# The last chunk's rows turned by TensorE, the early experts' loads on SP alone, and new ranks for the planner, in a fused mLSTM, FFN and MoE kernel

## The chip, the cores and the metric

The kernel runs on one core of a Trainium2 chip. The metric is the device time of one execution in microseconds. Of the kernel before there are three timed runs, with a median of 672.15 us (670.86 to 674.29), and one more execution with a profile.

## The reference

Three layers follow each other. With B = 4 sequences, H = 8 heads, S = 768 steps and D = 40 there are 3072 tokens of 320 values.

```
# 1. mLSTM, per batch and head, over the steps t
m_new = max(f_t + m, i_t);  f' = exp(f_t + m - m_new);  i' = exp(i_t - m_new)
C = f' * C + i' * outer(v_t, k_t);   n = f' * n + i' * k_t
y_t = sigmoid(o_t) * (C @ q_t) / max(|n . q_t|, 1)
x = y as [3072, 320]
# 2. FFN: w_in [320, 2048], w_out [2048, 320]
h = x @ w_in;   x = (h * sigmoid(h)) @ w_out
# 3. MoE, top 1 of 8 experts: w1 [8, 320, 1024], w2 [8, 1024, 320]
e = argmax(x @ w_gate);   p = softmax(x @ w_gate)[e]
out = p * (relu(x @ w1[e]) @ w2[e])
```

All values are float32.

## The kernel before, in words

**Tiles.** The sequence is cut into six chunks of 128 steps, and a unit is one chunk of one sequence: unit t = 4c + b, so units 20 to 23 are the last chunk. A unit loads K, Q, V and the gates, makes scores and values on TensorE in the chunkwise form of the recurrence, and ends with a tile of 128 tokens, written as two f16 halves (a high and a low part) into `yy`. The FFN wants that tile turned, tokens along the free axis. `turned` (L624) does it: for t below 3 by six TensorE transposes (L636) and a copy (L638), else by one DMA transpose on SP's queue (L628). K and Q of all chunks but the first are turned by L628 too.

**FFN.** `l1(t, g)` takes a quarter of the 2048 columns in two halves of 16 products each (L1018, 128x512 of PSUM in all). ScalarE makes tanh of it (L1020), VectorE the gate product (L1022), ScalarE casts the high f16 part (L1025), and VectorE or GpSimd makes the low part (L1026). `l2(t, g)` then takes twelve products with `w_out` (L1047 to L1049) into one bank, and after the fourth quarter ScalarE moves the tile out (L1053).

**Route.** After each chunk `route(c)` scales its four tiles into f16 rows (L1102 on ScalarE, L1105 on GpSimd, L1106 on VectorE), turns each row block by a DMA transpose on SP (L1110), takes the gate logits on TensorE (L1122), and finds for each token its expert and its place among that expert's tokens (up to L1151). GpSimd then sends the tokens' rows by indirect DMA (L1177) to their places in a table in HBM, `rows_x`.

**Experts.** A slot is 128 tokens of one expert: `fetch_slot` (L1252, L1253) brings them in turned by a DMA transpose, and `slot` multiplies them by the expert's w1 (L1279), applies relu (L1281, L1283), multiplies by w2 (L1292 to L1294), weights them (L1297) and writes them out (L1309). Seven slots of experts 0 to 2 are early: they hold tokens of the first five chunks alone and run beside the end of the FFN and the last route. Then come 18 static slots, and three extra slots whose expert is known only at run time. An expert's weights come in quarters. `load_e` (L1190) issues four DMAs for a quarter (L1201 to L1204, 704 KB in all) into a stage, of which there are two at first. ScalarE and VectorE convert the stage into f16 halves: L1215 and L1228 on ScalarE, L1219, L1223 and L1230 on VectorE. A quarter is named (e, g) below, expert and quarter. The issue of a load with a fixed expert may go on SP's queue or on ScalarE's.

**What sets the order.** The program is first recorded as operations with engine, duration, tiles read and written, and a rank (L1 to L281). A list scheduler then runs over all operations forward and backward eight times with these durations, and keeps the round with the earliest planned end. The instructions of every engine are emitted in the order of that plan. At run time each engine works off its own list in order, with semaphores between engines, and the queues of SP and ScalarE hold their DMA issues in the same order. The ranks of the operations are built from constants in `RK` (L28), so another constant or another duration can move any instruction of any engine.

**What the change touches.** `RK`; `turned`; the call of `turned` for K, Q and `yy` in `unit`; L1110 in `route`; the engine choice in `load_e`, by `load_all`; four of the planner's durations.

Of the kernel before, what the change touches and what calls it, by code (L numbers as in the profile page):

```python
# [25 lines left out]
SWG = 32.0  # L26
EX = 4
RK = dict(  # L28
    tiles=19.85, win=310.54, dwin=120.43, wout=56.12, dwout=-21.22, u0=-372.07, u1=-36.9, u2=-978.22, u3=-878.97,
    lead1=113.09, lead=1032.66, l1c=-437.46, l2c=-463.45, l2=-163.58, gates=-736.39, load=-73.54, state=-65.11, route=-284.86,  # L30
)


# [254 lines left out]
def mlstm_moe_kernel(ctx, tc, q, k, v, ig, fg, og, w_in, w_out, w_gate, w1, w2, out):  # L288
    nc = tc.nc
    B, H, S, D = q.shape  # L290
# [17 lines left out]
    def op(*args, **kw):  # L308
        plan[0].op(*args, **kw)
# [91 lines left out]
    we_b = []  # L401
# [219 lines left out]
    def src(x, c, b):  # L621
        return x[b, :, c * CH:(c + 1) * CH, :].rearrange("h p d -> p h d")

    def turned(t, a, z, n, rank):  # L624

        flat = a.ap[:, 0:n * 128] if len(a.ap.shape) == 2 else a.ap.rearrange("p x c -> p (x c)")
        if t >= B - 1:
            op("SP", 1300, lambda: sp.dma_start_transpose(out=z.ap, in_=flat), R=[a], W=[z], rank=rank,  # L628
               lag=2800, move=212 * n)
            return  # L630
        ps, kk = bank("at", 128, 512)
        ps = ps.bitcast(F16)[:, 0:n * 128].rearrange("p (x c) -> p x c", c=128)

        def go():
            for x in range(n):
                pe.transpose(ps[:, x, :], flat[:, x * 128:(x + 1) * 128], ident16)  # L636
        op("PE", 70 * n, go, R=[a, "ident"], W=[kk], rank=rank)
        op(AD, ad(128 * n), lambda m: (m.copy if m is ac else m.tensor_copy)(out=z.ap, in_=ps), R=[kk], W=[z], rank=rank)  # L638

    def unit(t):  # L640
# [42 lines left out]
        def whole_turned(a, z, r):  # L683

            flat = a.ap.rearrange("p h d -> p (h d)")
            ps, kk = bank("at", 128, 512)

            def go():
                for i in range(4):
                    x = slice(i * 128, (i + 1) * 128)  # L690
                    pe.transpose(ps[:, x], flat[:, x], ident)
            op("PE", 4 * 110, go, R=[a, "ident"], W=[kk], rank=r)
            op(AD, ad(512), lambda m: (m.copy if m is ac else m.tensor_copy)(out=single(z), in_=ps),
               R=[kk], W=[z], rank=r)

# [3 lines left out]
        if c == 0:  # L699
            whole_turned(kr, kT, p)  # L700
            whole_turned(qr, qT, p + 0.5)
        else:
            halves(kr.ap, kr, k4[:, :, 0::2, :], k4[:, :, 0, :], k4[:, :, 1, :], K, p)
            turned(t, K, kT, H, p)
            halves(qr.ap, qr, q4[:, :, 0:2, :], q4[:, :, 0, :], q4[:, :, 2, :], Q, p + 0.5)
            turned(t, Q, qT, H, p + 0.5)

        def exps(h, x):
            ac.activation(  # L709
# [3 lines left out]
        for g in range(2):  # L713
            if c == 0:
                ps, kk = bank("at", 128, 4, CH)

                def first(g=g, ps=ps):
                    pe.matmul(ps, idb.ap, mneg.ap, start=True, stop=False)
                    for j in range(4):
                        h = b * H + 2 * j + g  # L720
                        one = sel.ap[:, h:h + 1].to_broadcast([128, 128])
                        pe.matmul(ps[:, j, :], one, parts.ap, start=False, stop=False)
                        pe.matmul(ps[:, j, :], bparts.ap, one, start=False, stop=(j == 3))
                op("PE", 700, first, R=[idb, mneg, sel, parts, bparts], W=[kk], rank=p + g)
                op("ACT", act(512), lambda g=g, ps=ps: ac.activation(out=lam[g].ap, in_=ps, func=AF.Exp),
                   R=[kk], W=[lam[g]], rank=p + 2 + g)
            else:
                for j in range(4):
                    op("ACT", actp(128), lambda g=g, j=j: exps(4 * g + j, lam[g].ap[:, j, :]),
                       R=[("bias", 1)], W=[lam[g]], rank=p + 2 + g)  # L730
# [21 lines left out]
        if c == 0:  # L752
            def pairs():
                for j in range(4):
                    x = slice(j * 128, j * 128 + 128)
                    for g in range(2):
                        r = slice(64 * g, 64 * g + D)
                        pe.matmul(two[g][0][:, j, :], single(kT)[r, x], single(qT)[r, x], start=True, stop=True)  # L758
            op("PE", 1300, pairs, R=[kT, qT], W=[two[0][1], two[1][1]], rank=p + 6)
        for g in range(2):  # L760
            ps, kk = two[g]
            if c > 0:
# [45 lines left out]
        def denom():  # L808
# [18 lines left out]
           W=[yy], rank=p + 12)  # L827
        op("DVE", dve(320), lambda: ve.tensor_tensor(out=yl, in0=y, in1=yh, op=ALU.subtract),
           R=[kv], W=[yy], rank=p + 12)
        turned(t, yy, xt, 6, p + 12)  # L830
        if c < NC - 1:
            pw, kk = bank("at", 128, H, D1)
            ps = pw[0:D]
# [71 lines left out]
    def rest(mid, i, hi, lo, scale, keys, rk):  # L905

        flat = mid.ap if len(hi.shape) == 2 else mid.ap.rearrange("p (a b) -> p a b", a=hi.shape[1])
        op("PE", 220, lambda: pe.matmul(flat, less[i], hi, start=False, stop=True, skip_group_check=True),
           R=["less", *keys], W=[mid], rank=rk)
        op(AD, ad(512), lambda m: scaled(nc, m, lo, flat, scale), R=[mid], W=keys, rank=rk)  # L910

# [155 lines left out]
    def route(c, b0, b1, rk, dr):  # L1067
# [29 lines left out]
        for b in range(nb):  # L1097
            row = rows[b]
            r16 = row.ap.bitcast(F16)
            rb = rk + (0.3 + 0.3 * b) * dr  # L1100
            x = x2[:, b]
            op("ACT", actp(320), lambda b=b, r16=r16, x=x: ac.activation(  # L1102
                out=r16[:, 0:DM], in_=x, func=AF.Copy, scale=sc[:, b:b + 1]
            ), R=[xs[b], (kr, "sc")], W=[row], rank=rb)
            op("POOL", 250, lambda r16=r16: po.tensor_copy(out=r16[:, DM:384], in_=r16[:, 256:DM]), W=[row], rank=rb)  # L1105
            op("DVE", dve(320), lambda b=b, r16=r16, x=x: ve.scalar_tensor_tensor(  # L1106
                out=r16[:, 384:704], in0=x, scalar=sc[:, b:b + 1], in1=r16[:, 0:DM],
                op0=ALU.mult, op1=ALU.subtract,
            ), R=[xs[b], (kr, "sc")], W=[row], rank=rb, port=True)
            op("SP", 1300, lambda b=b, r16=r16: sp.dma_start_transpose(out=xr[b].ap, in_=r16[:, 0:768]),  # L1110
               R=[row], W=[xr[b]], rank=rb, lag=2800, move=1270)
        yield
        pl, kl = bank("at", 128, nb, E)

# [72 lines left out]
    stcount = [0]  # L1187
    stages = [stg_b]

    def load_e(e, g, dst, rk, lead, reg=None):  # L1190

        s = stages[0]
        t1, t2 = s[stcount[0] % len(s)]
# [4 lines left out]
        def fetch(m=sp):  # L1198
# [6 lines left out]
            else:  # L1205
# [3 lines left out]
                sp.dma_start(out=t1.ap[0:64, 2, :], in_=c.rearrange("e p f -> (e p) f"))  # L1209
                sp.dma_start(out=t1.ap[64:128, 2, :], in_=c.rearrange("e p f -> (e p) f"))  # L1210
                sp.dma_start(out=t2.ap, in_=d.rearrange("e (j p) d -> p (e j) d", p=128))
        op(("SP", "ACT") if reg is None else "SP", (2150, 2150) if reg is None else 3300, fetch,
           R=[] if reg is None else [("xreg", e)], W=[t1, t2],
           rank=rk - lead, lag=2500, move=2500, after=rk - lead - 10)
        op("ACT", act(768), lambda: ac.activation(out=o1.ap[:, 0:3, :], in_=t1.ap, func=AF.Copy, scale=SWE),  # L1215
# [15 lines left out]
            out=o2.ap[:, :, 1, :], in0=t2.ap, scalar=SWE, in1=o2.ap[:, :, 0, :], op0=ALU.mult, op1=ALU.subtract  # L1231
        ), R=[t2], W=[o2], rank=rk, port=True)

    def load_all(e, rk):
        for g in range(NG):
            load_e(e, g, we_b[e], rk - 18 + 2 * g, 20)


    scount = [0]
# [83 lines left out]
    for t in range(2, B):  # L1323
# [4 lines left out]
       rank=12)  # L1328
# [77 lines left out]
    end0 = pos(NTT) + 10  # L1406
    for n, (e, i) in enumerate(early):
        if e > 1 and e != early[n - 1][0]:
            load_all(e, end0 + 2 + TS * n)
        slot(i, we_b[e], end0 + 2 + TS * n)  # L1410


# [168 lines left out]
```

## Time and profile before

| what | us |
|---|---|
| median of three timed runs | 672.15 |
| the profiled execution, its own time | 669.95 |
| its span, from the first to the last instruction | 668.3 |
| TensorE busy | 619.5 (93%) |
| VectorE busy | 491.4 (74%) |
| ScalarE busy | 389.8 (58%) |
| GpSimd busy | 299.9 (45%) |

The time is read as the span plus 1.65 us around it. TensorE is the engine with the most work by far. Its busy time is the sum of the instructions at the clock that they ran at; the mean granted clock was 0.973 of full speed. The share of busy time is a mean over stages that differ: the attention and the FFN run together up to about 450 us, the early slots and the last route up to about 510, and after that the experts alone.

### The profile page before, as it was taken

What the parts mean: (1) busy time and instruction counts of PE and PEld (TensorE: products, weight loads), DVE (VectorE), ACT (ScalarE), POOL (GpSimd) and SP (SyncE); (2) the same over time, 40 slices, a digit from 0 to 9 for tenths busy, and PEclk for the clock granted to TensorE, in tenths of its full rate; (3) what the DMA queues carried; (4) which work ended last, traced back from release to release, by engine and by line L of the source; (5) the groups of instructions that cost most, each with busy time, mean ns of one, the idle gap of its engine ahead of it and who ended that gap; (6) DMA issues with size and microseconds to landing.
All of it is one profiled execution on the core that took longest, in us unless ns stands there. A gap on an engine that the chain in (4) does not pass through costs nothing.

```text
span 668.3 us, 21038 instructions
## 1 busy us (share of the span) xinstructions
PE 619.5 (93%) x8435; PEld 532.6 (80%) x8435; DVE 491.4 (74%) x1001; ACT 389.8 (58%) x804; POOL 299.9 (45%) x441
## 2 busy tenths in 40 slices
PE   3888999999899999999999999959799999999993
PEld 2677888888788878888888888838588888888882
DVE  6977886797889798898877887625169567676561
ACT  1657787877688686878776755434134445454340
POOL 4113456575577586876855743311042132223121
PEclk9996999999999999999999999969899999999997
DMA  8996687999999898997799544372734899878820
GB/s 183 273 224 147 147 151 133 194 250 162 192 170 196 140 152 154 181 183 134 158 148 165 147 120 101 118 144 41 149 120 114 192 227 258 178 223 205 200 68 15
DMA packets 273219, 107.84 MB, mean 161 GB/s; under 512 B 210229, under 2 KB 268792, under 8 KB 273112
## 3 DMA queue, kind: packets, MB, share of 16 engines
q1 hardware_dynamic: 257560, 84.75, 65.3%
q10 hardware_dynamic: 12672, 12.98, 7.2%
q0 software_dynamic: 2880, 8.68, 3.7%
q8 instruction: 68, 1.11, 0.7%
q14 instruction: 39, 0.32, 0.2%
HBM read 68.76 MB, written 12.38 MB: 121 GB/s over the span
## 4 chain that ended last, share of the span: by engine, by line
PE 70%; DVE 10%; DMA 9%; SPq 3%; issue 3%; ACT 3%; POOL 2%; ACTq 1%; POOLq 0%; DVEq 0%
PE PS L1018 18%; PE PS L1279 14%; PE PS L1049 6%; PE PS L1047 6%; PE PS L1048 6%; PE PS L1292 4%; PE PS L1294 4%; PE PS L1293 4%; DMA A<-A 4%; DMA A<-in_k_dram 2%; DVE A L768 1%; PE PS L766 1%; SPq L1252 1%; DVE A L1022 1%; PE PS L758 1%
## 5 line engine op out<-in xcount | busy, mean ns | idle before, releaser
L1018 PE MATMUL PS<-A,A 128*128 128x128 f16 x3072 | 196.4, 222 | 6.5 <-DVE A L1022 6.1
L1018 PEld LDWEIGHTS <-A 128*128 128x128 f16 x3072 | 182.7, 99 | 13.4 <-issue 8.5
L1279 PEld LDWEIGHTS <-A 128*128 128x128 f16 x1792 | 107.8, 98 | 6.4
L1279 PE MATMUL PS<-W,A 128*128 128x128 f16 x1664 | 107.1, 220 | 0.0
L1047 PE MATMUL PS<-A,A 128*128 128x320 f16 x344 | 103.5, 301 | 2.7 <-ACT A L1025 2.7
L1049 PE MATMUL PS<-A,A 128*128 128x320 f16 x344 | 103.5, 301 | 0.1
L1048 PE MATMUL PS<-A,A 128*128 128x320 f16 x344 | 103.5, 301 | 0.0
L1309 POOL DMA_INDIRECT out_dram<-W,sid x28 | 30.1, 1074 | 133.1 <-DVE W L1297 40.7
L1281 ACT ACTIVATE W<-PS 128x512 f16<-128x512 f32 x56 | 32.6, 593 | 87.5 <-PE PS L1279 40.9
L1020 ACT ACTIVATE A<-PS 128x512 f32<-128x512 f32 x96 | 56.5, 592 | 44.2 <-PE PS L1018 21.5
L1022 DVE SCALAR_TENSOR_TENSOR A<-A,PS 128x512 f32<-128x512 f32 x96 | 64.6, 678 | 20.7 <-ACT A L1020 20.1
L1292 PE MATMUL PS<-A,W 128*128 128x320 f16 x224 | 67.3, 300 | 4.9 <-DVE W L1297 4.9
L1283 DVE SCALAR_TENSOR_TENSOR W<-PS,W 128x512 f16<-128x512 f32 x56 | 38.0, 687 | 40.7 <-ACT W L1281 40.3
L1294 PE MATMUL PS<-A,W 128*128 128x320 f16 x224 | 67.3, 301 | 0.0
L1293 PE MATMUL PS<-A,W 128*128 128x320 f16 x224 | 67.3, 301 | 0.0
L1025 ACT CAST A<-A 128x512 f16<-128x512 f32 x86 | 52.4, 614 | 15.7 <-DVE A L1022 11.3
L1026 POOL TENSOR_TENSOR A<-A 128x512 f16<-128x512 f32 x32 | 38.9, 1216 | 48.0 <-ACT A L1025 47.7
L709 ACT ACTIVATE A<-A,bias_t 128x128 f32<-128x128 f32 x160 | 56.9, 393 | 3.2 <-POOL A L668 3.2
L768 DVE SCALAR_TENSOR_TENSOR A<-PS,A 128x512 f32<-128x512 f32 x48 | 32.5, 684 | 18.7 <-PE PS L766 13.5
L1049 PEld LDWEIGHTS <-A 128*128 128x128 f16 x344 | 33.8, 98 | 14.0 <-DVE A L1026 0.7
L1026 POOL TENSOR_TENSOR A<-A,A 128x512 f16<-128x512 f32 x26 | 33.4, 1286 | 24.2 <-ACT A L1025 24.1
L777 POOL TENSOR_TENSOR A<-A 128x512 f16<-128x512 f32 x27 | 33.1, 1228 | 24.7 <-ACT A L775 24.5
(269 smaller groups left out, 1299.6 us busy)
## 6 DMA issues: line engine op xcount, KB each, us to landing
A<-lam_d SPq DMA_DIRECT2D x40, 256.0 KB
SG<-in_moe_w_dram SPq DMA_DIRECT2D x20, 320.0 KB
A<-in_moe_w_out_dram SPq DMA_DIRECT2D x10, 512.0 KB
SG<-in_moe_w_dram SPq DMA_DIRECT2D x20, 256.0 KB
SG<-in_moe_w_dram ACTq DMA_DIRECT2D x14, 320.0 KB
A<-in_moe_w_in_dram SPq DMA_DIRECT2D x8, 512.0 KB
A<-in_k_dram SPq DMA_DIRECT2D x24, 160.0 KB
A<-in_q_dram SPq DMA_DIRECT2D x24, 160.0 KB
```

The lines of the kernel that those rows point to most:

```text
L709: ac.activation(out=lam[h // 4].ap[:, h % 4, :], in_=x, func=AF.Exp, bias=bias_t[:, c, b * H + h:b * H + h + 1])
L1018: pe.matmul(ps[:, f, :], a, x, start=(n == 0), stop=(n == len(terms) - 1))
L1020: op("ACT", act(512), lambda: ac.activation(out=th.ap, in_=ps, func=AF.Tanh, scale=0.5 * HS), R=[kk], W=[th], rank=rk)
L1022: op("DVE", dve(512), lambda: ve.scalar_tensor_tensor(out=th.ap, in0=th.ap, scalar=1.0, in1=ps, op0=ALU.add, op1=ALU.mult), R=[kk], W=[th] ...
L1026: op(DP, dp(512), lambda m: m.tensor_tensor(out=G.ap[:, 1], in0=th.ap, in1=G.ap[:, 0], op=ALU.subtract), R=[th], W=[G], rank=rk + 2, port= ...
L1047: pe.matmul(ps, gh, w[:, 0, :], start=(f == 0), stop=False)
L1048: pe.matmul(ps, gh, w[:, 1, :], start=False, stop=False)
L1049: pe.matmul(ps, gl, w[:, 0, :], start=False, stop=(f == NF - 1))
L1279: pe.matmul(ps[:, jj, :], l, m, start=(n == 0), stop=(n == len(terms) - 1))
L1292: pe.matmul(ps, hh[:, 0, f % 4, :], x[:, 0, :], start=(f == 0), stop=False)
L1293: pe.matmul(ps, hh[:, 0, f % 4, :], x[:, 1, :], start=False, stop=False)
L1294: pe.matmul(ps, hh[:, 1, f % 4, :], x[:, 0, :], start=False, stop=(f == NF2 - 1))
```

## The change

1. `turned` is told by its caller which way to go. For K and Q it is always the DMA, as before; for `yy` it is TensorE when t is below B - 1 = 3, as before. The rows of a route now go through `turned` too: the last route's four blocks by TensorE (six transposes and a copy each), the earlier routes' by a DMA transpose as before.
2. A load may be issued by ScalarE only when its caller says `late`. Experts 0 and 1, and expert 2 (loaded among the early slots), are now issued by SP alone; experts 3 to 7 by either, as before.
3. All constants of `RK` but one have new values, and four durations of the planner for TensorE have them: 540 for the four f32 transposes (440 before), 740 for the first gate products (700), 1170 for the pairs of scores (1300), 300 for the prefix product (220), all in ns.

```diff
 RK = dict(
-    tiles=19.85, win=310.54, dwin=120.43, ..., route=-284.86,
+    tiles=19.85, win=353.85, dwin=106.13, ..., route=-479.0,
 )
...
-    def turned(t, a, z, n, rank):
-
-        flat = a.ap[:, 0:n * 128] if len(a.ap.shape) == 2 else a.ap.rearrange("p x c -> p (x c)")
-        if t >= B - 1:
+    def turned(a, flat, z, n, rank, by_pe):
+
+        if not by_pe:
             op("SP", 1300, lambda: sp.dma_start_transpose(out=z.ap, in_=flat), R=[a], W=[z], rank=rank,
                lag=2800, move=212 * n)
             return
...
-            op("PE", 4 * 110, go, R=[a, "ident"], W=[kk], rank=r)
+            op("PE", 540, go, R=[a, "ident"], W=[kk], rank=r)
...
-            turned(t, K, kT, H, p)
+            turned(K, K.ap[:, 0:H * 128], kT, H, p, False)
...
-        turned(t, yy, xt, 6, p + 12)
+        turned(yy, yy.ap.rearrange("p x c -> p (x c)"), xt, 6, p + 12, t < B - 1)
...
-            op("SP", 1300, lambda b=b, r16=r16: sp.dma_start_transpose(out=xr[b].ap, in_=r16[:, 0:768]),
-               R=[row], W=[xr[b]], rank=rb, lag=2800, move=1270)
+            turned(row, r16[:, 0:768], xr[b], 6, rb, last)
...
-    def load_e(e, g, dst, rk, lead, reg=None):
+    def load_e(e, g, dst, rk, lead, reg=None, late=False):
...
-        op(("SP", "ACT") if reg is None else "SP", (2150, 2150) if reg is None else 3300, fetch,
+        op(("SP", "ACT") if late else "SP", (2150, 2150) if late else 2150 if reg is None else 3300, fetch,
...
-    def load_all(e, rk):
+    def load_all(e, rk, late=True):
         for g in range(NG):
-            load_e(e, g, we_b[e], rk - 18 + 2 * g, 20)
+            load_e(e, g, we_b[e], rk - 18 + 2 * g, 20, late=late)
...
-            load_all(e, end0 + 2 + TS * n)
+            load_all(e, end0 + 2 + TS * n, False)
```

The order of the instructions is shown at three places; line numbers are those of each kernel, and after the change most lines stand one to three lower.

The first is ScalarE's list at the FFN's last tiles. `SG` is a stage of expert weights, `PS` a bank of PSUM; L1020 is the tanh and L1025 the cast of an l1. Before:

```order
605 L1201 DMA SG<-in_moe_w_dram 128x2x256
606 L1202 DMA SG<-in_moe_w_dram 64x256
607 L1203 DMA SG<-in_moe_w_dram 64x256
608 L1204 DMA SG<-in_moe_w_dram 128x2x320
609 L1020 ACTIVATE A_72<-PS 128x512
610 L1025 CAST A_73<-A_73 128x512
611 L1201 DMA SG<-in_moe_w_dram 128x2x256
612 L1202 DMA SG<-in_moe_w_dram 64x256
613 L1203 DMA SG<-in_moe_w_dram 64x256
614 L1204 DMA SG<-in_moe_w_dram 128x2x320
615 L1025 CAST A_73<-A_72 128x512
616 L1020 ACTIVATE A_73<-PS 128x512
```

After, ScalarE's list there has L1019 and L1024 for the same two, and L1213 and L1226 for the conversions of a stage:

```order
576 L1024 CAST A_73<-A_72 128x512
577 L1213 ACTIVATE A_70<-SG 128x768
578 L1226 ACTIVATE A_70<-SG 128x2x320
579 L1019 ACTIVATE A_73<-PS 128x512
580 L1024 CAST A_73<-A_73 128x512
581 L1019 ACTIVATE A_72<-PS 128x512
582 L1024 CAST A_73<-A_72 128x512
583 L1052 ACTIVATE X_93<-PS 128x320
584 L1019 ACTIVATE A_73<-PS 128x512
585 L1213 ACTIVATE A_70<-SG 128x768
586 L1024 CAST A_73<-A_73 128x512
587 L1226 ACTIVATE A_70<-SG 128x2x320
```

The issues of the quarters (2,2) and (2,3) have left this list; the conversions of (2,0) and (2,1) stand between the last l1's casts.

The second is ScalarE's list at the last route: L1281 is a slot's relu, L1102 makes a route's rows, and the loads are those of (3,0) and (3,1). Before:

```order
628 L1281 ACTIVATE W_96<-PS 128x512
629 L1102 ACTIVATE A_72<-X_93,sc_114 128x320 x4
630 L1281 ACTIVATE W_96<-PS 128x512 x2
631 L1201 DMA SG<-in_moe_w_dram 128x2x256
632 L1202 DMA SG<-in_moe_w_dram 64x256
633 L1203 DMA SG<-in_moe_w_dram 64x256
634 L1204 DMA SG<-in_moe_w_dram 128x2x320
635 L1201 DMA SG<-in_moe_w_dram 128x2x256
636 L1202 DMA SG<-in_moe_w_dram 64x256
637 L1203 DMA SG<-in_moe_w_dram 64x256
638 L1204 DMA SG<-in_moe_w_dram 128x2x320
639 L1281 ACTIVATE W_96<-PS 128x512 x2
```

After (L1101 the rows, L637 the copies of the turned blocks, L1279 the relu):

```order
593 L1199 DMA SG<-in_moe_w_dram 128x2x256
594 L1200 DMA SG<-in_moe_w_dram 64x256
595 L1201 DMA SG<-in_moe_w_dram 64x256
596 L1202 DMA SG<-in_moe_w_dram 128x2x320
597 L1101 ACTIVATE A_72<-X_93,sc_114 128x320 x4
598 L1213 ACTIVATE A_70<-SG 128x768
599 L637 COPY A_71<-PS 128x768 x2
600 L1279 ACTIVATE W_96<-PS 128x512
601 L1226 ACTIVATE A_70<-SG 128x2x320
602 L637 COPY A_71<-PS 128x768 x2
603 L1199 DMA SG<-in_moe_w_dram 128x2x256
604 L1200 DMA SG<-in_moe_w_dram 64x256
```

The load of (3,0) moved from behind the rows to ahead of them, that of (3,1) stands behind the four new copies, and conversions of expert 2 lie between.

The third is SP's list from the fetches of the early slots on (a transpose L1252 out of `rows_x` and a small DMA L1253 each; L1110 is a turned row block). Before:

```order
295 L1253 DMA xm_130<-rows_x 128x2
296 L1252 DMA_TRANSPOSE A_72<-rows_x 128x6x128
297 L1253 DMA xm_131<-rows_x 128x2
298 L1252 DMA_TRANSPOSE A_72<-rows_x 128x6x128
299 L1253 DMA xm_132<-rows_x 128x2
300 L1110 DMA_TRANSPOSE A_71<-A_72 128x6x128 x4
301 L1201 DMA X_93<-in_moe_w_dram 128x2x256
```

After (L1250 and L1251 are the fetch, L1199 to L1202 a load):

```order
294 L1250 DMA_TRANSPOSE W_96<-rows_x 128x6x128
295 L1251 DMA xm_129<-rows_x 128x2
296 L1199 DMA SG<-in_moe_w_dram 128x2x256
297 L1200 DMA SG<-in_moe_w_dram 64x256
298 L1201 DMA SG<-in_moe_w_dram 64x256
299 L1202 DMA SG<-in_moe_w_dram 128x2x320
300 L1250 DMA_TRANSPOSE W_96<-rows_x 128x6x128
301 L1251 DMA xm_128<-rows_x 128x2
302 L1199 DMA SG<-in_moe_w_dram 128x2x256
303 L1200 DMA SG<-in_moe_w_dram 64x256
304 L1201 DMA SG<-in_moe_w_dram 64x256
305 L1202 DMA SG<-in_moe_w_dram 128x2x320
```

The four row blocks are gone from SP's list, and the loads of (2,1) and (2,2) stand between the fetches, behind the third and the fourth of the seven; (2,3) follows behind the sixth.

## Rows read from the trace of the kernel before

**Rows 1.** The page's part 1: busy time, share of span, instructions.

```profile
PE 619.5 (93%) x8435; PEld 532.6 (80%) x8435; DVE 491.4 (74%) x1001; ACT 389.8 (58%) x804; POOL 299.9 (45%) x441
```

**Rows 2.** Windows: stretch, length, busy PE, PEld, DVE, ACT, POOL, clock, DMA, GB/s.

```profile
20.00:60.00 40.00, 33.24 (x254) 26.30 (x252) 35.29 (x67) 25.66 (x50) 6.21 (x11) 0.85 1.03 241
60.00:130.00 70.00, 69.83 (x964) 60.84 (x964) 54.30 (x104) 53.47 (x117) 41.00 (x62) 0.99 0.75 149
130.00:300.00 170.00, 163.11 (x2614) 142.97 (x2612) 145.67 (x309) 130.00 (x303) 115.57 (x142) 1.00 0.99 177
436.60:451.20 14.60, 6.69 (x44) 4.59 (x42) 5.13 (x7) 5.21 (x9) 3.33 (x4) 0.65 0.67 135
473.60:481.10 7.50, 2.63 (x17) 1.96 (x17) 1.75 (x3) 1.09 (x2) 1.02 (x1) 0.82 0.70 218
481.10:656.60 175.50, 175.50 (x2258) 151.50 (x2255) 115.33 (x224) 73.32 (x116) 44.11 (x77) 1.00 0.69 171
```

**Rows 3.** Waits of TensorE, 420 to 490 us: us in total, times, longest.

```profile
PE PS L1018 <- DVE A L1022: 5.1, 1, 5.1
PE PS L1292 <- DVE W L1297: 4.9, 1, 4.9
PE PS L1047 <- ACT A L1025: 2.7, 1, 2.7
```

**Rows 4.** Timeline of ScalarE and its queue (ACTq): start, us, idle before and releaser.

```profile
433.09 0.38 ACTq L1201 DMA_DIRECT2D SG<-in_moe_w_dram  x1
438.53 0.48 ACTq L1202 DMA_DIRECT2D SG<-in_moe_w_dram  x1
...
440.40 0.60 ACT L1020 ACTIVATE A<-PS 128x512 f32<-128x512 f32 x1 [10.74 <-issue]
...
445.72 0.62 ACT L1025 CAST A<-A 128x512 f16<-128x512 f32 x1 [4.21 <-DMA SG<-in_moe_w_dram]
```

**Rows 5.** Chain of waits around the second hole: start, us, what.

```profile
467.59 7.22 DMA A<-A
474.83 0.47 ACTq L1202
...
476.69 0.61 ACT W L1281
...
478.52 0.42 PE PS L1292
```

**Rows 6.** The chain again: one 128x320 matmul near 448 and near 640 us.

```profile
448.44 0.27 PE PS L1047
...
639.94 0.14 PE PS L1292
```

**Rows 7.** Timeline: a slot's fetch on SP's queue, a load on ScalarE's.

```profile
429.85 1.23 SPq L1252 DMA_TRANSPOSE W<-rows_x  x1
431.12 0.56 SPq L1253 DMA_DIRECT2D xm<-rows_x  x1
...
464.34 0.38 ACTq L1201 DMA_DIRECT2D SG<-in_moe_w_dram  x1
...
466.36 0.69 ACTq L1204 DMA_DIRECT2D SG<-in_moe_w_dram  x1
```

**Rows 8.** Lines L636 and L638 (durations min/median/max), and six transposes in the timeline.

```profile
L636 PE MATMUL PS<-ident,A x18: 219/300/315, 30.7 to 76.7; 128*128 128x128 f16 x18
...
L638 ACT COPY A<-PS x2: 798/816/834, 32.1 to 54.6; 128x768 f16<-128x768 f16 x2
...
76.41 0.50 PE L636 MATMUL PS<-ident,A 128*128 128x128 f16 x6
```

**Rows 9.** The chain of waits at the start: tile 1's K.

```profile
32.20 5.98 DMA A<-in_k_dram
```

**Rows 10.** VectorE's last conversion of a quarter; the chain's next L1279.

```profile
648.89 0.42 DVE L1223 SCALAR_TENSOR_TENSOR A<-SG,A 64x256 f16<-64x256 f32 x1
...
650.27 0.89 PE PS L1279 x16
```

More of the change, by code (lines that the diff above doesn't have):

```diff
@@ L28 @@
 RK = dict(
-    tiles=19.85, win=310.54, dwin=120.43, wout=56.12, dwout=-21.22, u0=-372.07, u1=-36.9, u2=-978.22, u3=-878.97,
-    lead1=113.09, lead=1032.66, l1c=-437.46, l2c=-463.45, l2=-163.58, gates=-736.39, load=-73.54, state=-65.11, route=-284.86,
+    tiles=19.85, win=353.85, dwin=106.13, wout=100.9, dwout=-28.38, u0=-480.22, u1=-100.63, u2=-1015.81, u3=-688.79,
+    lead1=67.84, lead=1075.92, l1c=-561.79, l2c=-315.25, l2=-159.96, gates=-935.97, load=-59.28, state=-85.71, route=-479.0,
 )
@@ L703, in unit @@
             halves(kr.ap, kr, k4[:, :, 0::2, :], k4[:, :, 0, :], k4[:, :, 1, :], K, p)
-            turned(t, K, kT, H, p)
+            turned(K, K.ap[:, 0:H * 128], kT, H, p, False)
             halves(qr.ap, qr, q4[:, :, 0:2, :], q4[:, :, 0, :], q4[:, :, 2, :], Q, p + 0.5)
-            turned(t, Q, qT, H, p + 0.5)
+            turned(Q, Q.ap.rearrange("p h c -> p (h c)"), qT, H, p + 0.5, False)
         def exps(h, x):
@@ L723, in first @@
                         pe.matmul(ps[:, j, :], bparts.ap, one, start=False, stop=(j == 3))
-                op("PE", 700, first, R=[idb, mneg, sel, parts, bparts], W=[kk], rank=p + g)
+                op("PE", 740, first, R=[idb, mneg, sel, parts, bparts], W=[kk], rank=p + g)
                 op("ACT", act(512), lambda g=g, ps=ps: ac.activation(out=lam[g].ap, in_=ps, func=AF.Exp),
@@ L758, in pairs @@
                         pe.matmul(two[g][0][:, j, :], single(kT)[r, x], single(qT)[r, x], start=True, stop=True)
-            op("PE", 1300, pairs, R=[kT, qT], W=[two[0][1], two[1][1]], rank=p + 6)
+            op("PE", 1170, pairs, R=[kT, qT], W=[two[0][1], two[1][1]], rank=p + 6)
         for g in range(2):
@@ L907, in rest @@
         flat = mid.ap if len(hi.shape) == 2 else mid.ap.rearrange("p (a b) -> p a b", a=hi.shape[1])
-        op("PE", 220, lambda: pe.matmul(flat, less[i], hi, start=False, stop=True, skip_group_check=True),
+        op("PE", 300, lambda: pe.matmul(flat, less[i], hi, start=False, stop=True, skip_group_check=True),
            R=["less", *keys], W=[mid], rank=rk)
```

## The prediction

> **What bounds the kernel now.** I began with the page's first part: TensorE is busy for 619.5 of 668.3 us [rows 1], so 48.8 us of idle is all that can be won without faster matmuls, plus what the lower clock costs around it. The windows put that idle in its places [rows 2]. From 20 to 60 us TensorE idles 6.8 us, from 130 to 300 us 6.9 us, from 436.6 to 451.2 us 7.9 us, from 473.6 to 481.1 us 4.9 us. From 481.1 to 656.6 us it idles not at all. The rest is the first 20 us and the 11.7 us tail, in which the last rows are weighted and written; the change leaves both alone.
>
> The two late holes are single stalls, not many small ones: in the waits of TensorE from 420 to 490 us there are three rows, each with one wait [rows 3]. ScalarE's timeline says why. It starts a DMA issue (L1201, a quarter of expert weights) at 433.09, gets the next piece out at 438.53, and only at 440.40 does the next activation L1020, the tanh of an l1, with 10.74 us idle before it put down to "issue" [rows 4]. ScalarE runs its queue in order, so a DMA that can't be issued holds the arithmetic behind it. The next load does it again: 4.21 us before the cast L1025 at 445.72. The second hole is read from the chain of waits: the transposes of the last chunk's rows by DMA land 7.22 us after 467.59, at 474.81; then ScalarE issues L1202 of another quarter at 474.83, reaches the relu L1281 at 476.69, and TensorE gets its operand at 478.5 [rows 5]. ScalarE's load stood behind a transfer of SP's queue with which it has no data in common; what holds it is the transfers issued before it. This is one cause in two places: a load on ScalarE's queue, issued while SP has slow transposes under way.
>
> **The clock.** After such a hole the matmuls run at the lower level: the chain gives a 128×320 matmul 0.27 us there (448.44) and 0.14 elsewhere (639.94) [rows 6], which are the 1.2 and the 2.4 GHz level. The granted clock is 0.65 over the first hole's window and 0.82 over the second's [rows 2]. The first window holds 6.69 us of TensorE work; were all of it at half clock, 3.3 us of it would be extra, and the 4.8 us after the second wait (446.4 to 451.2) give 2.4 alone. I take 3.0. In the second, 0.82 over 7.5 us is 2.7 us of half clock, nearly all of it work after the wait, so 1.3 extra. First stall 7.9 + 3.0 = 10.9 us, second 4.9 + 1.3 = 6.2 us.
>
> **The change part by part.**
>
> *Loads of experts 0 to 2 on SP alone.* ScalarE's order shows it: in the sequence of L1019 and L1024 for the last tiles no issue is left. What held ScalarE for 10.74 and 4.21 us is gone there: −10.9. The price moves to SP, whose queue now has three loads between the slot fetches. A fetch takes SP 1.9 us (two issues, 429.85 to 431.68); the four issues of a load that nothing holds took ScalarE 2.7 us (464.34 to 467.05) [rows 7]. The first fetch can't begin before 429.85, when the tokens' rows have landed, so seven fetches and three loads take 7 × 1.9 + 3 × 2.7 = 21.4 us and the last is out near 451; before, the loads on ScalarE were out at 445.7. The first early slots want experts loaded long before; quarter (2,1) has to be converted ahead of the last l1's cast. It stands behind three fetches: begun at 435.5, out at 438, landed at 444 by the 5.98 us of the K transfer in [rows 9], and somewhat sooner for the three pieces that the first conversion wants. Counted through the new order of TensorE at the present pace, ScalarE comes to it near 444. That cover is thin, 0 to 2 us. Here *DMA: Bandwidth & Descriptors* in the Trainium skill speaks, under "Issuing engines are not separate DMA queues": all issuers share the same DMA engines, and several of them save only the sequencer's time to initiate, usually small. By that page alone, giving up ScalarE as an issuer would cost SP the 2.7 us a load and free no more of ScalarE's, and of the first hole 5.4 us would go for two loads instead of 10.9. The trace disagrees for this place, where one load held ScalarE for 7 us [rows 4].
>
> *The last rows turned by TensorE.* It removes four DMA transposes from SP (1.2 us each) and the wait of 7.22 us on their landing [rows 5]: −6.2 with the clock, if no other transfer holds ScalarE there. ScalarE still issues quarter (3,0) right ahead of the rows L1101 and (3,1) behind the turned copies. (3,0) went out in 2.7 us at 464.3 before [rows 7]; the transfers ahead of it in the new order, the last fetches and (2,3), should have landed. The attention's tiles are turned as they were: 3 to 23 are turned by DMA, 0 to 2 by TensorE.
> It adds 24 transposes on TensorE. Six took 0.50 us at 76.41 [rows 8], so 24 take 2.0 us, on TensorE's path whole, as nothing is idle there once the stalls are gone. From above: 24 × 0.30, the median one by itself [rows 8], is 7.2 us, if they don't overlap; the row of six is the nearer, since the 24 also come in sixes. Four copies of 128×768 follow, 0.8 us each [rows 8], 3.3 us on ScalarE, which the slots' matmuls hide: from TensorE's done transposes to the logits there is slot work of more than 3 us. If that cover is gone, up to 0.8 us for the last copy.
> A rule of the Trainium skill speaks against this edit: *TensorE: Matmul & The Clock Gate*, "Part 4: PE-mode transpose", gives about 275 ns for such a transpose within a kernel and says that it doesn't count as busy for the clock. By it the 24 would take 6.6 us, an estimate from that page, and the sum would be 5 us worse. The trace has six in 0.50 us [rows 8] and a granted clock of 0.99 from 60 to 130 us around them [rows 2], so I keep 2.0.
>
> *The ranks.* Every instruction is ordered anew. At the start, tile 1's K, whose DMA of 5.98 us issued at 32.20 TensorE's chain waits for [rows 9], now stands at row 17 of SP's queue instead of 27, ten issues earlier. Of the 6.8 us of idle from 20 to 60 us I take 2 back; 5 would be nearly all of it. Against it SP now has tile 3's turned output ahead of tile 5's loads, so SP waits for the values of tile 3 with those loads behind it; that could cost 1 to 3 us. So −2, from −5 to +3. From 130 to 300 us the idle is 6.9 us in many waits under 1 us each; the new order sets the attention tiles some microseconds later against the FFN and their loads earlier against their use. I take −3, from −6 to +5, as the window before it (69.83 of 70 us [rows 2]) shows that the same loop can run with nearly none. For new small waits of an order that has not been timed, +3 where the stalls were (0 to 8; 8 is one wait like the first hole's 5.1 [rows 3] with its clock part of 3).
>
> **Sum** against the profiled execution's 669.95 us: −10.9 − 6.2 + 2.0 − 2 − 3 + 3 = −17.1, so 652.9. That execution is 2.2 us under the median 672.15, so 655 against the median, and this is my forecast. With all unknowns at their good ends: −10.9 − 6.2 + 2.0 − 5 − 6 = −26.1, 646. At their bad ends: −17.1 + 7.2 + 3 + 5 + 8 = +6, 678.
>
> **The rivals.**
> - *A stall stays in part* (0.13). ScalarE still has issues among the rows and copies of the last route: (3,0) ahead, (3,1) behind. If one is held by SP's fetches, half the first stall's or all of the second's 6.2 us remains: 661. For it: every issue that held ScalarE did so behind SP's transposes [rows 4, 5], and the seven fetches are now spread over a longer time. Against it: the four row transposes are gone.
> - *The end is bound by loads* (0.10). The extra slots' last converted quarter ends at 648.89 + 0.42 = 649.31, and the L1279 group after it starts at 650.27 [rows 10]: 1 us of slack. If the weights come only 10 us earlier while TensorE comes 17, it waits about 6: 661. Against it: those loads wait for stages that TensorE's own progress frees, so they move along.
> - *Nothing comes of it* (0.07): the row transfers only hid another wait, such as the route's logits coming late behind the conversions, and both holes stay in the trace under another name. 672.
> - *Slower* (0.07): SP becomes the holder. If SP's loads (2,1), (2,2), (2,3) are held between the fetches as ScalarE's was (7.2 instead of 2.7 us each), the last is 13.5 us late. The conversions L1213 stand in ScalarE's queue ahead of the last cast and of the route's copies, so TensorE loses these 13.5 us and the clock after two holes again (3.0 + 1.3); with 2.0 for the transposes and 3 for new waits that is 22.8 against the 17.1 + 5 won, 673, and 678 if start and middle win nothing. It costs from the point where (2,1) lands after 444, and is a loss from 17 us of delay on.
> - The forecast's own case: 0.63.
>
> **How the numbers follow.** 0.5% here is 3.4 us, about what a measurement can tell from no change. Faster: 0.63 + 0.13 + 0.10 = 0.86. Same 0.07, slower 0.07. The range is 645 to 668: below, the good ends of start and middle; above, the two partial cases (661) with the bad ends of the start added. What it leaves out is the last two cases, 0.14, and little below 645.
>
> **What would show it.** The waits from 420 to 490 us without "L1018 from L1022" and "L1292 from L1297" above 1 us; ScalarE's idle of "issue" there under 3 us; granted clock 0.95 or more in both stretches. L635 at about 0.5 us per six. TensorE's idle from 20 to 60 us below 5. I am wrong if a conversion L1213 or L1226 waits on a DMA issued by SP with TensorE idle behind it, if TensorE waits in the last 140 us, or if the idle in the first 300 us grows by more than the 5 that I took from it.

## The result and the profile after

| | kernel before | kernel after |
|---|---|---|
| median, us | 671.50 (668.77 to 674.29, 4 runs) | 651.53 (645.65 to 658.05, 4 runs) |
| ratio | | 0.9673 (0.9591 to 0.9756) |
| profiled execution: own time, span | 669.95, 668.3 | 650.66, 648.8 |

The kernel is 20 us faster; 655 was forecast, with a range of 645 to 668. The ratios here and below leave out runs in a slower state of the chip: that of 658.05 us here, two of the six of a_again and one of the six of a_01_late2. The profile after is read by the same views. Its part 1, and the windows that answer to [rows 2] (the last three cover the places of the two holes and the experts):

```profile
PE 609.4 (94%) x8459; PEld 526.3 (81%) x8459; DVE 497.6 (77%) x1003; ACT 391.9 (60%) x806; POOL 297.5 (46%) x441
```

```profile
20.00:60.00 40.00, 33.12 (x348) 27.64 (x349) 37.24 (x71) 26.95 (x57) 8.41 (x13) 0.83 0.89 206
60.00:130.00 70.00, 70.00 (x1004) 61.17 (x1003) 57.16 (x117) 54.69 (x123) 40.59 (x64) 1.00 0.82 166
130.00:300.00 170.00, 161.50 (x2547) 141.77 (x2546) 141.44 (x293) 125.37 (x285) 110.34 (x139) 0.99 0.98 168
...
437.00:461.00 24.00, 24.00 (x330) 21.26 (x329) 14.65 (x30) 13.21 (x23) 4.09 (x10) 1.00 0.52 139
461.00:481.00 20.00, 20.00 (x297) 17.80 (x295) 11.56 (x35) 7.78 (x13) 6.88 (x10) 1.00 0.44 142
481.00:637.00 156.00, 155.99 (x1970) 133.90 (x1969) 104.33 (x191) 67.04 (x106) 38.06 (x66) 1.00 0.76 180
```

Both holes are gone: from 437 to 637 us TensorE is busy for 199.99 of 200 us at full clock. The waits of TensorE from 420 to 490 us, three rows before [rows 3], are now an empty list. Before 300 us it is not better: idle from 130 to 300 us is 8.5 us (6.9 before), of which one wait is the most:

```profile
PE PS L765 <- DMA A<-A: 4.3, 1, 4.3
PE PS L784 <- DMA A<-A: 1.3, 1, 1.3
PE PS L1148 <- DVE A L827: 1.3, 1, 1.3
```

Idle alone doesn't account for the clock, so I use a lag: the start of a TensorE instruction less the work ahead of it in its list, each kind of work at the median start-to-start of the undisturbed stretches of before. A lag that grows is time lost, to waits or to half clock. The work is 607.3 us before and 609.0 after (the transposes). The lag in us, at times of each trace; the last three columns are experiments:

| at | before | after | b_loads_sp | b_loads31_sp | a_01_late |
|---|---|---|---|---|---|
| 90 | 21.7 | 14.4 | 18.8 | 20.3 | 16.0 |
| 190 | 26.7 | 17.3 | 26.6 | 26.9 | 17.2 |
| 215 | 26.9 | 23.2 | 26.8 | 27.2 | 17.2 |
| 300 | 30.7 | 25.9 | 30.0 | 30.4 | 19.5 |
| 420 | 31.4 | 28.5 | 30.0 | 30.4 | 20.8 |
| 460 | 42.8 | 28.3 | 30.0 | 30.4 | 20.5 |
| 500 | 49.4 | 28.2 | 36.0 | 30.4 | 20.6 |
| 640 | 49.4 | 28.4 | 37.0 | 30.8 | 23.1 |

Between before and after: start −7.3 (at 90), middle +4.4 (90 to 420: 9.7 became 14.1), first hole −11.6, second hole and what follows −6.5, more work +1.7; together −19.3, against −19.5 of the spans.

### The profile page after: what moved, and what is told of

It is laid out like the page before. It is cut to its first block, busy times and chain, and to the rows that moved or that the text cites. A ratio compares the mean times of both kernels' runs of the same rounds, so it can differ in the third digit from the quotient of the medians.

```text
span 648.8 us, 21082 instructions
## 1 busy us (share of the span) xinstructions
PE 609.4 (94%) x8459; PEld 526.3 (81%) x8459; DVE 497.6 (77%) x1003; ACT 391.9 (60%) x806; POOL 297.5 (46%) x441
## 4 chain that ended last, share of the span: by engine, by line
PE 84%; DVE 6%; DMA 3%; issue 2%; ACT 2%; POOL 1%; SPq 0%; POOLq 0%; DVEq 0%; ACTq 0%
PE PS L1017 24%; PE PS L1277 15%; PE PS L1048 7%; PE PS L1046 7%; PE PS L1047 7%; PE PS L1292 5%; PE PS L1290 5%; PE PS L1291 5%; DMA A<-A 2%; PE PS L796 1%; PE PS L765 1%; DMA SG<-in_moe_w_dram 1%; PE PS L1120 1%; PE PS L907 1%; DVE A L1025 1%
## 5 line engine op out<-in xcount | busy, mean ns | idle before, releaser
L1017 PEld LDWEIGHTS <-A 128*128 128x128 f16 x3072 | 181.0, 99 | 7.9 <-issue 2.0
L1277 PEld LDWEIGHTS <-A 128*128 128x128 f16 x1792 | 107.5, 98 | 6.5
L1019 ACT ACTIVATE A<-PS 128x512 f32<-128x512 f32 x96 | 57.0, 594 | 50.9 <-PE PS L1017 46.6
L1279 ACT ACTIVATE W<-PS 128x512 f16<-128x512 f32 x56 | 33.2, 594 | 80.4 <-PE PS L1277 49.9
L1281 DVE SCALAR_TENSOR_TENSOR W<-PS,W 128x512 f16<-128x512 f32 x56 | 38.4, 688 | 34.4 <-ACT W L1279 33.4
L1024 ACT CAST A<-A 128x512 f16<-128x512 f32 x86 | 52.5, 612 | 13.4 <-DVE A L1021 12.9
L1025 POOL TENSOR_TENSOR A<-A,A 128x512 f16<-128x512 f32 x31 | 39.1, 1260 | 42.1 <-ACT A L1024 40.6
L1025 POOL TENSOR_TENSOR A<-A 128x512 f16<-128x512 f32 x31 | 37.6, 1213 | 32.2 <-ACT A L1024 32.1
L1048 PEld LDWEIGHTS <-A 128*128 128x128 f16 x344 | 33.6, 98 | 14.5 <-POOL A L1025 1.4
L1047 PEld LDWEIGHTS <-A 128*128 128x128 f16 x344 | 33.6, 98 | 10.0
L1046 PEld LDWEIGHTS <-A 128*128 128x128 f16 x344 | 33.6, 98 | 9.8
```

The costliest lines, as they stand in the source:

```text
L1017: pe.matmul(ps[:, f, :], a, x, start=(n == 0), stop=(n == len(terms) - 1))
L1019: op("ACT", act(512), lambda: ac.activation(out=th.ap, in_=ps, func=AF.Tanh, scale=0.5 * HS), R=[kk], W=[th], rank=rk)
L1025: op(DP, dp(512), lambda m: m.tensor_tensor(out=G.ap[:, 1], in0=th.ap, in1=G.ap[:, 0], op=ALU.subtract), R=[th], W=[G], rank=rk + 2, port= ...
L1046: pe.matmul(ps, gh, w[:, 0, :], start=(f == 0), stop=False)
L1047: pe.matmul(ps, gh, w[:, 1, :], start=False, stop=False)
L1048: pe.matmul(ps, gl, w[:, 0, :], start=False, stop=(f == NF - 1))
```

## The experiments

Kernels whose names begin with b_ come from before, those with a_ from after. Where "its own order" is said, the plan is made as in that kernel and then only the named operations change engine or place, by two lists that the emitting loop looks up (`ENG`: operation to issuing engine; `MOVE`: operation, and the one before which it now stands). So nothing else is reordered.

**b_loads_sp: the first hole.** The loads (2,2) and (2,3), operations 2378 and 2383, go to SP.

```diff
+ENG = {2378: 'SP', 2383: 'SP'}
```

> The kernel before with its own order, where the loads of the quarters (2,2) and (2,3) are issued by SP at the place in the plan where ScalarE issued them; nothing else moves. Theory (ScalarE is held by issues that wait for earlier DMAs): the first hole goes, TensorE's waits of 5.1 us (L1018) and 2.7 us (L1047) and their half clock, so -10.9 us, about 660.6, ratio 0.984; the second hole of 4.9 us stays. Rival (the quarters' data, or the DMA engines, are late whoever issues): the hole stays, as a wait on a DMA into SG; time within 1% of before. Second rival (SP's fetches are delayed by the two loads, and the early slots wait): waits at L1279, between 660 and 670.

Measured: 658.79 us beside 669.67 of before, −10.9 us; ratio 0.9822 (0.9738 to 0.9905). TensorE's waits from 420 to 490 us are one row:

```profile
PE PS L1292 <- DVE W L1297: 4.4, 1, 4.4
```

The first hole is gone to the last microsecond (lag 30.0 at 420 and at 460), the second is where it was. So the issue on ScalarE's queue was the hole; the data come in time from SP. SP isn't held in ScalarE's place: (2,2) goes out ahead of the first fetch, (2,3) behind the second, and neither has to wait for a fetch to land (timeline of SP's queue):

```profile
425.45 0.37 SPq L1201 DMA_DIRECT2D SG<-in_moe_w_dram  x1
...
427.72 0.54 SPq L1204 DMA_DIRECT2D SG<-in_moe_w_dram  x1
428.70 1.22 SPq L1252 DMA_TRANSPOSE W<-rows_x  x1
...
434.18 0.53 SPq L1204 DMA_DIRECT2D SG<-in_moe_w_dram  x1
```

What ScalarE waited for stands in the trace of before. In this program the DMAs of SP and ScalarE share eight completion semaphores (signals that a DMA has landed), and an issue waits until the earlier DMA on its semaphore has landed, whichever engine issued that. L1202 of 438.53 waited for a fetch's transpose that SP issued at 433.62 and that landed at 438.51. At the second hole L1201 of 474.31 and L1202 of 474.83 waited for the third and the fourth row block, which landed at 474.29 and 474.81.

**b_loads_pool: must it be SP?** The same two loads go to GpSimd.

```diff
+ENG = {2378: 'POOL', 2383: 'POOL'}
```

> The kernel before with its own order, where the loads (2,2) and (2,3) are issued by GpSimd at the place where ScalarE issued them; SP's queue is untouched. Theory (ScalarE alone is what the held issue stops, and its place in the list is the cause): the first hole goes as it did with SP as issuer, -9 to -11 us, 659 to 661, second hole stays. Rival (it was SP's own queue that had to carry them, so that they come after the fetches): the loads' data come late or GpSimd's low parts of l1 are held instead, and TensorE waits 3 us or more at L1047 to L1049 near 440 to 450; 663 to 670.

Measured: 658.88 us beside 667.66, ratio 0.9853 (0.9818 to 0.9889). The lag is 27.8 at 420 and at 460; the only row of waits at the two holes is the second hole's:

```profile
PE PS L1292 <- DVE W L1297: 5.3, 1, 5.3
```

So SP is not what cures it. GpSimd isn't held either: its eight issues go out one behind the other, on semaphores that only GpSimd's DMAs use (timeline of GpSimd):

```profile
425.52 0.80 POOL L1201 DMA_DIRECT2D SG<-in_moe_w_dram  x1
...
429.92 0.77 POOL L1204 DMA_DIRECT2D SG<-in_moe_w_dram  x1
```

In neither of the two experiments was an issue of these loads held, so they don't show yet what a held one does on another queue; the next one does.

**b_loads31_sp: the second hole.** The load (3,1) goes to SP as well.

```diff
+ENG = {2378: 'SP', 2383: 'SP', 2480: 'SP'}
```

> The kernel before with its own order, where the loads (2,2), (2,3) and (3,1) are issued by SP at their places; the last chunk's rows are still turned by DMA. Theory (the issue held ScalarE in both holes): both go, -17.1 us, about 654.4, ratio 0.975, although no row is turned by TensorE. Rival (the second hole is the rows' DMA transposes themselves, whose landing the logits wait for): the second hole stays at the logits L1122 with 4 to 5 us of wait, time about 661.

Measured: 652.42 us, −17.3, ratio 0.972 (0.9641 to 0.9799). The list of waits from 420 to 490 us is empty and the lag stays 30.4, although the four row blocks still go through SP's queue as DMA transposes, and although the load behind them is held as before, now on SP (timeline of SP's queue):

```profile
451.12 5.44 SPq L1110 DMA_TRANSPOSE A<-A  x4
456.61 1.23 SPq L1201 DMA_DIRECT2D SG<-in_moe_w_dram  x1
458.81 0.49 SPq L1202 DMA_DIRECT2D SG<-in_moe_w_dram  x1
462.02 0.47 SPq L1203 DMA_DIRECT2D SG<-in_moe_w_dram  x1
```

L1203 gets out 3 us after L1202; TensorE waits for nothing that stands behind it on SP. Three issuers changed, with no row turned by TensorE and no new rank, give 17.3 us beside the 20 of the whole change; the intervals of the ratios (0.972 and 0.9673) overlap for the most part.

**a_rows_dma: the turned rows, in the new order.**

```diff
-            for x in range(n):
+            for x in range(0 if as_dma else n):
...
-        op(AD, ad(128 * n), lambda m: (m.copy if m is ac else m.tensor_copy)(out=z.ap, in_=ps), R=[kk], W=[z], rank=rank)
+        op(AD, ad(128 * n), lambda m: sp.dma_start_transpose(out=z.ap, in_=flat) if as_dma else (m.copy if m is ac else m.tensor_copy)(out=z.ap, in_=ps), R=[kk], W=[z], rank=rank)
```

> The kernel after with its own order, where the four row blocks of the last route are turned by a DMA transpose on SP, issued at the place of the four copies; the 24 TensorE transposes are left out. Theory (only the held issue mattered): TensorE saves 1.8 us of transposes; the logits come 4 x 1.2 us of issue and some 4 to 7 us of landing later than with the copies, and TensorE's list has slot work only for a part of that, so a wait of 3 to 6 us at the logits L1120 and half clock after it: +2 to +6 us, 653.5 to 657.5. Rival (turning the rows on TensorE is worth nothing or costs): -2 us, 649.5. Rival (it is the main gain of the second hole): +6 or more, 658, with ScalarE's load (3,1) held again.

Measured: 657.47 us, 6 above the 651.5 of after and 5 above a_early_act beside the same before (next experiment); ratio to before 0.9778 (0.9695 to 0.9861). TensorE's waits from 420 to 490 us, and the chain before the logits:

```profile
PE PS L1120 <- DMA A<-A: 6.9, 1, 6.9
```

```profile
457.84 1.09 SPq L637
458.98 0.81 SPq L1199
...
461.99 6.18 DMA A<-A
468.21 0.59 PE PS L1120 x16
```

The last block is issued at 461.99, behind a load, and lands 6.18 us later. From 420 to 500 us the lag grows by 8.0 here: 6.9 of wait and the clock after it, less what the transposes would have taken. So in the order of after the turned rows are worth 5 to 6 us, though in the order of before they were worth nothing once the load was away. There, in b_loads31_sp, the blocks are issued from 451.12 to 456.56 and the logits begin at 463.64, 7 us of slot work later; here TensorE is at the logits at 461.3 (468.21 − 6.9). Some 3 us of that are the place behind the load (458.98 to 461.99), which an order made for DMA would not have.

**a_early_act: the held issue, put back.** The loads (2,2) and (2,3) go from SP to ScalarE.

```diff
+ENG = {2382: 'ACT', 2387: 'ACT'}
```

> The kernel after with its own order, where the loads (2,2) and (2,3) are issued by ScalarE at the places where SP issued them. Theory (an issue on ScalarE's queue beside SP's slot fetches is held by them): the first hole comes back, ScalarE idle 4 to 11 us put down to issue near 436 to 448 and TensorE waiting 5 us or more behind it with half clock after: +6 to +11 us, 657 to 662. Rival (the new order of the conversions is what closed the hole, whoever issues): within 3 us of the kernel after.

Measured: 652.41 us, no difference from after (0.9695 against 0.9673); the rival was right. The issue is held again (timeline of ScalarE):

```profile
437.54 0.47 ACTq L1199 DMA_DIRECT2D SG<-in_moe_w_dram  x1
438.05 0.53 ACTq L1200 DMA_DIRECT2D SG<-in_moe_w_dram  x1
439.56 0.48 ACTq L1201 DMA_DIRECT2D SG<-in_moe_w_dram  x1
441.20 0.38 ACTq L1202 DMA_DIRECT2D SG<-in_moe_w_dram  x1
441.67 0.60 ACT L1019 ACTIVATE A<-PS 128x512 f32<-128x512 f32 x1 [4.34 <-DMA SG<-in_moe_w_dram]
```

but TensorE's only wait from 420 to 470 us is 0.4 us. The hold is shorter, 4.34 us beside 10.74, and behind the issue stands L1019, whose operand TensorE has ready only at 440.88, 0.8 us before the hold ends (in after, where nothing holds it, it starts at 441.49, after a wait for TensorE). A held issue costs what it keeps waiting behind it, not what it lasts.

**a_01_late: the middle.** In after, SP issues the loads (0,1) and (0,2) from 167.20 to 173.3 us, in front of the K and Q transposes of units 10 and 11; those of unit 11 are the 4.3 us wait. The experiment moves the loads (871, 958) and their conversions; in its trace they go out at 346 and 359 us. Timeline of SP's queue, after, and the chain at that wait:

```profile
167.20 0.47 SPq L1199 DMA_DIRECT2D SG<-in_moe_w_dram  x1
...
171.26 2.06 SPq L1202 DMA_DIRECT2D SG<-in_moe_w_dram  x1
173.44 1.26 SPq L627 DMA_TRANSPOSE A<-A  x1
...
188.84 5.31 SPq L627 DMA_TRANSPOSE A<-A  x2
```

```profile
188.84 7.77 DMA A<-A
...
196.65 0.38 PE PS L765 x4
```

```diff
+MOVE = [(871, 1974), (872, 1957), (874, 1957), (873, 1965), (958, 2047), (959, 2023), (961, 2023), (960, 2024)]
```

> The kernel after with its own order, where the loads (0,1) and (0,2) and their conversions stand some 190 us later, among the DMAs at 355 and 367 us. Theory (the new waits near 180 to 200 us come from the two loads that SP now issues at 167 to 173 us, in front of the K and Q transposes of units 10 and 11): the waits of 4.3 and 1.3 us and their half clock go, -5 to -6 us, 646, unless a later tile waits instead. Rival (that stretch is bound by the transposes and loads of attention anyway): the wait moves to another unit before 300 us, within 2 us of the kernel after.

Measured: 644.91 us, ratio to before 0.9659 (0.9616 to 0.9703). By the ratio that is no more than after's 0.9673, as the kernel before was faster beside it too (667.66 us); the lag says more. The lag is the same as after's at 190 us and then stays: 17.2 at 215 (23.2 after), 20.8 at 420 (28.5). The transposes of unit 11 are issued at 183.81, 5 us sooner. Since the executions of after vary by 1% among themselves, both were run again beside the same kernel before:

> The kernel after once more, unchanged, beside a_01_late2: both theories 647 to 653.

> a_01_late once more, beside the kernel after. Theory (the two loads of expert 0 on SP at 167 to 173 us cost the kernel after 5 us): 4 to 7 us below a_again, and TensorE's lag the same up to 170 us and 5 us smaller at 215. Rival (the difference lay between the executions of the kernel after): within 2 us of a_again.

Measured, as medians of the runs that the ratios count: a_again 653.6 us, 0.9721 (0.9667 to 0.9774); a_01_late2 647.0, 0.9634 (0.9581 to 0.9687). The two differ by 6.7 us, and the intervals overlap at their edges. The lag of a_01_late2 is 18.2 at 215 and 23.1 at 420. From 90 to 215 us the lag grows by 1.2 and 2.5 us where the two loads stand late, and by 6 to 9 us in three profiles that have them near 167 us (after, a_early_act, a_rows_dma). So the loads there cost time, and this is the fastest version, by about 6 us.

**a_01_act: is it SP's time, or the DMA engines'?** The loads (0,1) and (0,2) stay at their places and go to ScalarE.

```diff
+ENG = {871: 'ACT', 958: 'ACT'}
```

> The kernel after with its own order, where the loads (0,1) and (0,2) are issued by ScalarE at the places in the plan where SP issues them, so that the same bytes move at nearly the same time. Theory (SP's time to issue is what runs out there): as good as moving them away, -4 to -6 us. Rival (the DMA engines' time runs out, their share is 1.0 there): no gain, the waits for the K and Q transposes stay. Second rival (ScalarE is held by the issues): TensorE waits for ScalarE between 165 and 190 us, +2 us or more.

Measured: 655.71 us, 0.9847 (0.9817 to 0.9877), no gain. The second rival happened, so the first question stays open: the waits for unit 11's transposes are gone from the list, but TensorE comes to them some 8 us later. The profiled execution is the fastest of the five (649.38). ScalarE's timeline, and the wait of TensorE that it made:

```profile
162.66 0.46 ACTq L1199 DMA_DIRECT2D SG<-in_moe_w_dram  x1
...
166.42 0.47 ACTq L1201 DMA_DIRECT2D SG<-in_moe_w_dram  x1
167.22 0.37 ACTq L1202 DMA_DIRECT2D SG<-in_moe_w_dram  x1
167.64 0.23 ACT L1131 ACTIVATE le<-ld 128x32 f32<-128x32 f32 x1 [6.39 <-DMA A<-in_q_dram]
```

```profile
PE PS L842 <- DVE A L767: 7.0, 1, 7.0
```

It is the first hole's mechanism at a third place, near 165 us: L1199 waited for a DMA of SP's that landed at 162.64, L1201 for one that landed at 166.40, L1202 for one at 167.20.

**h_start: does the start's gain last?** The first 401 operations (`HEAD`, with their engines) stand as in after, the rest as in before.

```diff
+        seq = HEAD + [x for x in seq if x[0] not in first]
```

> The kernel before where the first 401 operations of the plan, to about 85 us, stand in the order of the kernel after, and the rest in its own. Theory (the start's gain of 5 to 7 us is given back before 300 us, where the attention's DMAs set the pace): TensorE's lag is 5 us smaller at 90 us and within 2 us of before at 300 us, time 668 to 672. Rival (the start's gain is real and lasts): -5 us or more, 665.

Measured: 676.41 us, 1.0135 (1.0074 to 1.0197). Inconclusive: the seam has a wait of its own, 7.2 us of L908 for ScalarE, and the lag goes from 15.9 at 90 us to 24.6 at 130. Whether the start's gain would last can't be read from it.

**b_ranks and a_old_ranks: the parts as the planner sees them.** In b_ranks before has the new RK and the four durations; in a_old_ranks after has the old ones.

```diff
-    tiles=19.85, win=310.54, dwin=120.43, ...
+    tiles=19.85, win=353.85, dwin=106.13, ...
...
-            op("PE", 4 * 110, go, R=[a, "ident"], W=[kk], rank=r)
+            op("PE", 540, go, R=[a, "ident"], W=[kk], rank=r)
```

> The kernel before with the new constants of RK and the four new durations alone; the planner then puts 22 loads on ScalarE, among them five of experts 0 and 1 and the quarters (2,1), (2,3) beside SP's fetches. Theory (an issue on ScalarE beside SP's slow transposes is what costs): holes of 3 to 10 us with idle of ScalarE put down to issue in two or three places, no gain over before, 664 to 680. Rival (the ranks are what made the kernel faster): 655 or less.

> The kernel after with the old constants of RK and the four old durations: loads of experts 0 to 2 on SP alone, last rows by TensorE, and the planner then has ScalarE issue its first load with (4,2). Theory (the rule on the loads is the gain, the ranks are worth 2 to 3 us): no hole above 2 us at 430 to 480, the start as in the kernel before (lag about 20 at 90 us), 650 to 657. Rival (without the new ranks the two loads of SP and the fetches collide elsewhere): a wait of 5 us or more on a DMA, 660 or more.

Measured: b_ranks 662.15 us, 0.985 (0.9793 to 0.9907); a_old_ranks 658.92, 0.9785 (0.9734 to 0.9837), beside 672.04 of before. Both miss what I expected. The first is better than the 664 to 680 forecast: the holes are there, but small. ScalarE is held for 7.78 us near 430 and TensorE's list has other work for most of it:

```profile
430.48 0.48 ACTq L1202 DMA_DIRECT2D SG<-in_moe_w_dram  x1
435.19 0.51 ACTq L1203 DMA_DIRECT2D SG<-in_moe_w_dram  x1
...
436.38 0.62 ACT L1025 CAST A<-A 128x512 f16<-128x512 f32 x1 [7.78 <-DMA xm<-rows_x]
```

```profile
PE PS L1047 <- ACT A L1025: 2.1, 1, 2.1
```

The lag at 90 us is 16.7 in b_ranks and 19.3 in a_old_ranks: the start belongs to the ranks. At 460 it is 30.0 and 29.2, where before has 42.8, so either part alone closes most of the first hole. Then it grows to 35.7 and 36.5 by 640, a growth that after doesn't have and that my 650 to 657 for a_old_ranks left out; which of the later waits is whose stays open. The two parts alone save 9.9 and 13.1 us, 23.0 in sum, and both together 18.4 beside the same before (a_again) and 20 in the first runs. That fits parts which close the same holes, but the 3 to 5 us between are no more than the noise of three such differences.

## Why the prediction was right, point by point

- **First hole, −10.9.** Right in mechanism and size for the kernel before: b_loads_sp took 10.9 us off by that alone, and the lag of before grew by 11.4 there. The prediction's estimate by the Trainium skill, *DMA: Bandwidth & Descriptors*, "Issuing engines are not separate DMA queues", was 5.4 us; the runs give double, as ScalarE lost the time in waiting for landings and not in issuing. But a_early_act shows that in the new order the loads could have stayed on ScalarE: it is also the new order that closes the hole.
- **Second hole, −6.2.** Right in size (6.6 by the lag), wrong in what removes it. I named the rows' transposes; it is ScalarE's load behind them. That load waited for their landing, through a shared semaphore. With the load away the rows may go by DMA (b_loads31_sp), unless an order like the new one leaves no work in front of the logits (a_rows_dma).
- **The 24 transposes, +2.0.** They took 1.83 us, in the timeline of after:

```profile
456.55 0.83 PE L635 MATMUL PS<-ident,A 128*128 128x128 f16 x12
459.01 0.50 PE L635 MATMUL PS<-ident,A 128*128 128x128 f16 x6
460.24 0.50 PE L635 MATMUL PS<-ident,A 128*128 128x128 f16 x6
```

  The granted clock is 1.00 around them. The 6.6 us that the prediction estimated by the Trainium skill, *TensorE: Matmul & The Clock Gate*, "Part 4: PE-mode transpose", did not come.
- **SP's thin cover, 0 to 2 us.** Enough: (2,1) is issued from 431.44, ScalarE converts it at 441.98 without a wait. The landing was not late, and the new waits of +3 didn't come either (lag 28.5 at 420, 28.2 at 500).
- **Start, −2.** Too small. The two profiles differ by 7.3 at 90 us; four profiles in the order of before (18.8 to 21.7, mean 20.0) and six in that of after (14.4 to 16.0, mean 15.3) by 4.7. I looked for it in the idle, which is the same (6.8 and 6.9 us from 20 to 60), so the sign that I had named, idle below 5 us, did not come. It lies in the clock. The means of the clock column over the whole window, 0.85 before and 0.83 after, can't show it, as the column reads 1.00 in before where the matmuls still start at half the rate (last section). Windows of before, and then of after, from 50 to 60 us:

```profile
50.00:55.00 5.00, 3.67 (x23) 2.37 (x23) 4.58 (x9) 4.95 (x10) 0.24 (x1) 0.50 1.18 205
55.00:60.00 5.00, 4.53 (x34) 3.78 (x33) 4.96 (x11) 3.75 (x9) 2.19 (x4) 0.50 0.83 181
```

```profile
50.00:55.00 5.00, 4.57 (x38) 3.87 (x38) 4.85 (x11) 4.11 (x10) 1.08 (x2) 0.66 0.50 131
55.00:60.00 5.00, 5.00 (x81) 4.54 (x79) 4.97 (x9) 3.76 (x8) 0.95 (x2) 1.00 0.14 22
```

  57 matmuls at the 1.2 GHz level there before, 119 after, most of them at 2.4. That the earlier loads of tile 1 keep TensorE fed is how I read it; no run tested that alone.
- **Middle, −3.** The wrong sign: +4.4. The step that failed is "I take −3, … as the window before it shows that the same loop can run with nearly none". I counted what the loads cost SP at the last chunk only, and not where else the early loads of expert 0 and 1 now stand on SP's queue. Two of them in front of the K and Q transposes cost 5 us and more; a_01_late gives it back.
- **The sum**, −17.1, was nearer to −19.5 than its terms: start and middle erred by 5.3 and 7.4 us with opposite signs, and the +3 for new waits did not come. That the total is near is in that part luck. None of the rivals came: no partial hole, no wait in the last 156 us, no load on SP that TensorE waited for after 420 us. The slower rival's mechanism, SP as the holder, did appear, at 180 us and for one unit.

## What to carry to other kernels

A DMA issue that has to wait stops every instruction behind it on its engine's queue. Put loads on a queue where they don't wait for slow transfers of another engine, or behind which nothing urgent stands, and look first at an engine's idle that is put down to "issue" or to a DMA that it doesn't read. Then change only the issuer, in the old order, before reordering anything: here three issuers gave 17.3 of the 20 us. And when work moves to another queue, walk through that queue over the whole span, not only at the place where the old stall was.

## What the runs showed of the hardware that was not expected

The clock column is 1.00 from 10 to 45 us in before, but matmuls of 128 columns start 0.11 us apart until 41.4 us and 0.07 at 41.5: in this trace the column doesn't show the level up to the first change that it records.

```profile
41.05 0.31 PE L722 MATMUL PS<-A 128*128 128x128 bf16 x1
41.16 0.31 PE L723 MATMUL PS<-A 128*128 128x128 bf16 x1
...
41.48 0.24 PE L722 MATMUL PS<-A 128*128 128x128 bf16 x1
41.55 0.22 PE L723 MATMUL PS<-A 128*128 128x128 bf16 x1
```

The four DMAs of a load are held each by itself. In [rows 4] the first goes out at 433.09, when a small DMA of a fetch has landed at 433.01, and the second at 438.53, when a transpose has landed at 438.51; the third and the fourth follow without a wait. In a_01_act all four wait, and the longest stop is ahead of the third (L1201, at 166.42).
